# Attention output copied out of its banks at once, with the reciprocals multiplied in later on GpSimd

## Chip, cores and metric

The kernel runs on one core of a Trainium2 chip. The metric is the device time of one execution in microseconds (us). Its engines are TensorE (PE), VectorE (DVE), ScalarE (ACT), GpSimd (POOL) and SyncE (SP); SP issues the DMAs. Matrix products are written to banks of PSUM, from which VectorE and ScalarE copy to SBUF.

## What is computed

Three layers follow one another: causal attention with a decay (4 batches, 8 heads, 576 positions, head size 64), a gated feed-forward layer (MoE1), and a routed layer of eight experts (MoE2). The change is in the attention:

```
scores = scale * np.matmul(q, k.transpose(0, 1, 3, 2))
log_f = np.log(np.clip(f, 0.0001, 1.0))
cum = np.cumsum(log_f, axis=-1)
decay = cum[:, :, :, None] - cum[:, :, None, :]
scores = np.where(causal, -1000000000.0, scores + decay)
scores = scores - np.max(scores, axis=-1, keepdims=True)
attn = np.exp(scores)
attn = attn / (np.sum(attn, axis=-1, keepdims=True) + 1e-09)
return np.matmul(attn, v).astype(np.float32)
```

## The kernel before

**Tiles and pairs.** The 32 heads of all batches are worked off as 16 pairs p (`NP`); the two heads of a pair lie on the two halves of the partitions. The 576 query rows of a head are cut into five tiles i (one of 64 rows and four of 128). The pair loop in `run` is a pipeline: while pair p is transposed and multiplied by v, the scores of pair p + 1 are made.

**One iteration.** It goes through four groups g. `tr(p, g, a)` transposes exponentials of head a into a bank `ps_t` (two buffers) and copies them to `ath`, on ScalarE for a = 0 (L174) and on VectorE for a = 1 (L172). The transposes are L157 in group 0, L160 in group 1, L163 and L164 in group 2, L168 and L169 in group 3. Between the groups, `qk(p + 1, i)` makes scores (L134), takes their row maximum on VectorE (L138) and the exponential with row sums on ScalarE (L145), and `av(p, g - 1)` (L184) multiplies by v into the two accumulating banks `avx` (512 columns) and `avy` (64 columns), of which there is one buffer each. `rb(p)` adds 1e-9 to the row sums (L190) and takes reciprocals (L191). They are needed along the free dimension of the output, which holds queries, so `rt(p)`, in group 1, transposes them on PE (L196), copies them (L198), writes them to DRAM (`rd`, L201) and reads them back spread over 64 partitions per head as `rb` (L203).

**End of a pair.** `xout(p)` multiplies both banks by `rb` on VectorE (L210, L211) and writes the product over `rb`. GpSimd then rounds it to `xth` (L213) and takes the remainder `xtl` (L214), the two parts that MoE1 reads.

**Other work in the loop.** From pair 5 on, every second pair decodes a sixth of MoE1's first weight group (`decode`: L285 on ScalarE, L286 to L288 on VectorE, L291, L292, L297 and L300 on GpSimd). In the last pair the decode of the next group begins, with its steps on VectorE (L294) and ScalarE (L299) where it has no GpSimd engine given. `decay`, ahead of the loop, computes the logarithms and their running sum and splits 8 times the sum into three bf16 parts `pc`, whose DMAs `dq` and `dk` feed the second product of L134.

**Order.** PE's order in the attention is that of the program (`manual_schedule(engines={PE})`). The order on the other engines is set by a scheduler when the program is built. Each engine then works strictly in its order.

Of the kernel before, what the change touches and what calls it, by code (L numbers as in the profile page):

```python
# [9 lines left out]
F32 = mybir.dt.float32  # L10
# [3 lines left out]
ACTF = mybir.ActivationFunctionType  # L14
ALU = mybir.AluOpType
# [4 lines left out]
B, H, S, D = 4, 8, 576, 64  # L20
# [15 lines left out]
class Attention:  # L36
# [46 lines left out]
    def decay(self, ft, cum, one, pc):  # L83
        nc = self.nc
        pc = pc.rearrange("p (r s) -> p r s", r=3)
        nc.vector.tensor_scalar(ft, ft, 0.0001, 1.0, op0=ALU.max, op1=ALU.min)
        nc.scalar.activation(ft, ft, ACTF.Ln)
        nc.vector.tensor_tensor_scan(cum, one, ft, 0.0, op0=ALU.mult, op1=ALU.add)
        nc.scalar.activation(ft[:1, :1], ft[:1, :1], ACTF.Exp)
        nc.vector.tensor_scalar_mul(cum, cum, 8.0)  # L90
        for r in range(3):
            nc.vector.tensor_copy(pc[:, r], cum)
            if r < 2:
                nc.vector.tensor_sub(cum, cum, pc[:, r])
        dq, dk = self.dec[0]
        nc.sync.dma_start(out=dq[61:67], in_=pc[:2])
        for a, o in enumerate((58, 67)):
            nc.sync.dma_start(out=dk[o:o + 3], in_=pc[a:a + 1])
        nc.sync.dma_start(out=self.cd, in_=pc)
# [105 lines left out]
    def xout(self, p):  # L205
        nc = self.nc
        ax, ay = self.X
        b, f = divmod(p, 4)
        xt = self.rbt
        nc.vector.tensor_mul(xt[:, 64:], ax, xt[:, 64:])  # L210
        nc.vector.tensor_mul(xt[:, :64], ay, xt[:, :64])  # L211
        sl = slice(b * S, (b + 1) * S)
        nc.gpsimd.tensor_copy(self.xth[:, f, sl], xt)  # L213
        nc.gpsimd.tensor_sub(self.xtl[:, f, sl], xt, self.xth[:, f, sl].bitcast(F32))  # L214
# [760 lines left out]
```

## Time and profile before

| | |
|---|---|
| three runs | 1047.93, 1048.97 and 1053.7 us |
| the profiled execution | 1053.49 us, span 1051.3 us |
| PE busy | 971.3 us, 92% of the span |
| VectorE busy | 604.6 us, 58% |
| ScalarE busy | 414.2 us, 39% |
| GpSimd busy | 208.6 us, 20% |
| mean granted TensorE clock | 0.963 of full speed |

The span runs from the first to the last instruction. Attention takes up about the first 265 us of it, MoE1 the stretch to about 740, MoE2 the rest. A granted clock of 1 is 2.4 GHz, one of 0.5 is 1.2 GHz. A busy share is a mean over all stages; what holds up one stage is seen in the waits and in the timeline of that stage.

### The profile page before, as it was taken

To read this page: it belongs to the slowest core of one execution; us is meant where nothing else is said; L and a number is where in the kernel's file an instruction comes from. 1 tells how busy PE (TensorE), PEld (TensorE's weight loads), DVE (VectorE), ACT (ScalarE), POOL (GpSimd) and SP (SyncE) were. 2 spreads that over 40 slices of the span, in tenths; PEclk is the share of its full clock that TensorE was granted. 3 is DMA by queue.
4 is the path that set the end of the run, shared out by engine and by line. 5 is a ranking of instruction groups with operands and counts; after the bars stand their busy time and mean duration, and the time that the engine had idled before them with its cause. 6 is when DMAs were issued, how large, how long until landed. Compare 5 with 4: busy or idle time off the path is not lost.

```text
span 1051.3 us, 16223 instructions
## 1 busy us (share of the span) xinstructions
PE 971.3 (92%) x6122; PEld 840.1 (80%) x6122; DVE 604.6 (58%) x1436; ACT 414.2 (39%) x903; POOL 208.6 (20%) x190
## 2 busy tenths in 40 slices
PE   4998898998999999999999999999899999879893
PEld 2544444444889999999999999989799999879693
DVE  4565655657763845945846645667775555442731
ACT  3655564554333412312313212333364544343631
POOL 1013222323210200201101100000125444532011
PEclk9998998889999999999999999999899999989997
DMA  6123222311220300201201100011485565652300
GB/s 200 64 88 108 95 98 84 114 57 53 72 61 21 101 1 23 98 1 41 80 1 61 41 1 1 31 51 52 154 273 172 188 208 190 221 185 68 114 38 27
DMA packets 53118, 92.93 MB, mean 88 GB/s; under 512 B 6032, under 2 KB 26894, under 8 KB 53039
## 3 DMA queue, kind: packets, MB, share of 16 engines
q1 hardware_dynamic: 47535, 77.70, 23.3%
q0 software_dynamic: 5504, 14.17, 3.9%
q8 instruction: 49, 0.80, 0.3%
q14 instruction: 30, 0.25, 0.1%
HBM read 82.19 MB, written 10.16 MB: 88 GB/s over the span
## 4 chain that ended last, share of the span: by engine, by line
PE 45%; issue 18%; DMA 12%; DVE 10%; POOL 9%; ACT 3%; SPq 0%; POOLq 0%; DVEq 0%; ACTq 0%
PE ps_g L336 21%; PE ps_y L354 12%; DMA rb<-rd 8%; PE ps_s L134 4%; PE avx L184 2%; POOL out L671 2%; DVE dt L287 2%; POOL gate L611 2%; POOL w L300 1%; POOL yg L611 1%; POOL b_r L611 1%; ACT e L145 1%; DVE ds L294 1%; DVE dt L288 1%; DMA rd<-rt 1%
## 5 line engine op out<-in xcount | busy, mean ns | idle before, releaser
L336 PE MATMUL ps_g<-xth,w 128*128 128x384 f32 (+1 forms) x1184 | 309.8, 332 | 1.5 <-DVE hs L341 1.5
L336 PEld LDWEIGHTS ps_g<-xth,w 128*128 128x128 f32 x1184 | 213.5, 188 | 2.8 <-DVE hs L341 2.2
L336 PE MATMUL ps_g<-xtl,w 128*128 128x384 f32 (+1 forms) x592 | 196.5, 332 | 0.0
L354 PE MATMUL ps_y<-hh,w 128*128 128x384 f32 (+1 forms) x592 | 161.1, 333 | 3.7 <-DVE y L360 2.1
L145 ACT ACTIVATE e<-e,mx 128x320 f32<-128x320 f32 (+4 forms) x160 | 88.2, 552 | 85.7 <-DVE mx L138 84.6
L630 PE MATMUL m_psg<-ygh,w 128*128 128x304 f32 x512 | 117.0, 310 | 1.6 <-ACT b_o L780 1.2
L645 PE MATMUL m_psy<-h2h,w 128*128 128x304 f32 x512 | 114.6, 306 | 0.0
L354 PEld LDWEIGHTS ps_y<-hh,w 128*128 128x128 f32 x592 | 107.1, 188 | 6.7 <-DVE y L360 3.9
L336 PEld LDWEIGHTS ps_g<-xtl,w 128*128 128x128 f32 x592 | 111.5, 188 | 0.1
L300 POOL TENSOR_TENSOR w<-ds,w 128x512 fp32r<-128x512 f32 x36 | 49.8, 1383 | 275.4 <-ACT w L299 274.9
L557 DVE TENSOR_TENSOR w<-raw,w 128x1024 fp32r<-128x1024 f32 x64 | 76.6, 1221 | 38.3 <-ACT w L556 22.7
L354 PE MATMUL ps_y<-hl,w 128*128 128x384 f32 (+1 forms) x296 | 97.9, 331 | 0.1
L343 ACT ACTIVATE hh<-hs 128x384 fp32r<-128x384 f32 (+1 forms) x74 | 38.2, 516 | 133.8 <-DVE hs L342 133.8
L341 DVE SCALAR_TENSOR_TENSOR hs<-hs,ps_g 128x384 f32<-128x384 f32 (+1 forms) x74 | 39.9, 540 | 87.1 <-ACT hs L340 87.1
L630 PEld LDWEIGHTS m_psg<-ygh,w 128*128 128x128 f32 x512 | 87.0, 192 | 2.1 <-ACT b_o L780 1.3
L645 PEld LDWEIGHTS m_psy<-h2h,w 128*128 128x128 f32 x512 | 85.5, 188 | 0.3
L134 PE MATMUL ps_s<-qk 64*128 64x288 f32 (+4 forms) x384 | 76.5, 471 | 5.6 <-DMA qk<-qk 5.3
L556 ACT ACTIVATE w<-raw 128x1024 fp32r<-128x1024 f32 x64 | 67.4, 1058 | 33.2 <-PE m_psg L630 13.0
L340 ACT ACTIVATE hs<-ps_g 128x384 f32<-128x384 f32 (+1 forms) x74 | 35.5, 479 | 109.1 <-PE ps_g L336 109.0
L630 PE MATMUL m_psg<-ygl,w 128*128 128x304 f32 x256 | 78.2, 305 | 0.2 <-DVE ygl L598 0.2
L138 DVE CUSTOM_DVE_ANT_0 e<-ps_s,mask 128x320 f32<-128x320 f32 (+4 forms) x160 | 62.5, 426 | 27.6 <-PE ps_s L134 25.7
L360 DVE TENSOR_TENSOR y<-ps_y,y 128x384 f32<-128x384 f32 (+1 forms) x124 | 67.0, 541 | 19.1 <-PE ps_y L354 18.2
(300 smaller groups left out, 1513.6 us busy)
## 6 DMA issues: line engine op xcount, KB each, us to landing
raw<-w SPq DMA_DIRECT2D x64, 512.0 KB
qk<-qk SPq DMA_DIRECT2D x16, 576.0 KB
raw<-mg SPq DMA_DIRECT2D x12, 512.0 KB
raw<-mv SPq DMA_DIRECT2D x12, 512.0 KB
raw<-mo SPq DMA_DIRECT2D x12, 512.0 KB
v<-vL SPq DMA_DIRECT2D x16, 320.0 KB
rb<-rd SPq DMA_DIRECT2D x16, 288.0 KB
yd<-yr SPq DMA_DIRECT2D x18, 256.0 KB
```

The lines of the kernel that those rows point to most:

```text
L134: nc.tensor.matmul(ps[a][b:, :n], x[s, q0:w], y[s, lo:hi], start=c == 0, stop=c == 1, tile_position=(64 * a, b))
L138: nc.vector.tensor_tensor_reduce(out=es[a][b:, lo:hi], in0=ps[a][b:, :n], in1=mask[b:, off + lo:off + hi], scale=-0.125, scalar=BIGF if pr ...
L145: nc.scalar.activation(es[a][b:, :w], es[a][b:, :w], ACTF.Exp, bias=prev[a][b:], scale=-1.0, accum_out=rs[b:, c:c + 1])
L300: nc.gpsimd.tensor_sub(lo, s3, hi.bitcast(F32))
L336: nc.tensor.matmul(ps[:, :n], w[:, k, fs], x[:, k], start=(k == 0 and c == 0), stop=(k == 3 and c == 2))
L354: nc.tensor.matmul(ps[:, :n], w[:, f, ds], h[:, f, :n], start=(f == 0 and c == 0), stop=(f == 1 and c == 2))
L360: nc.vector.tensor_add(y, ps[:, :n], y)
L556: nc.scalar.activation(hi, r, ACTF.Copy)
L557: nc.vector.tensor_sub(lo, r, hi.bitcast(F32))
L611: self.pmark = self.nc.gpsimd.indirect_dma_start(out=dst, out_offset=None, in_=src[:, :], in_offset=bass.IndirectOffsetOnAxis(ap=ix, axis= ...
L630: nc.tensor.matmul(ps[:, :C], w[:, k, fs], x[:, k], start=(k == 0 and c == 0), stop=(k == 3 and c == 2))
L645: nc.tensor.matmul(self.P[e][d][:, :C], w[:, f, ds], h[:, f], start=(u == 0 and f == 0 and c == 0), stop=(u == 3 and f == 1 and c == 2))
```

## The change

`xout` no longer multiplies out of the banks. ScalarE copies `avx` and VectorE copies `avy`, unnormalised, into a tile `xt` of its own, and GpSimd multiplies `xt` by `rb` before it rounds and subtracts as before. The pool of `rb` also holds `xt`, two buffers each. In `decay` the scaling by 8 is merged into the split, which takes four VectorE operations in place of six.

```
-        nc.vector.tensor_scalar_mul(cum, cum, 8.0)
-        for r in range(3):
-            nc.vector.tensor_copy(pc[:, r], cum)
-            if r < 2:
-                nc.vector.tensor_sub(cum, cum, pc[:, r])
+        nc.vector.tensor_scalar_mul(pc[:, 0], cum, 8.0)
+        nc.vector.scalar_tensor_tensor(cum, cum, 8.0, pc[:, 0], op0=ALU.mult, op1=ALU.subtract)
+        nc.vector.tensor_copy(pc[:, 1], cum)
+        nc.vector.tensor_sub(pc[:, 2], cum, pc[:, 1])
...
-        xt = self.rbt
-        nc.vector.tensor_mul(xt[:, 64:], ax, xt[:, 64:])
-        nc.vector.tensor_mul(xt[:, :64], ay, xt[:, :64])
+        xt = self.xp.tile([128, S], F32, name="xt")
+        nc.scalar.activation(xt[:, 64:], ax, ACTF.Copy)
+        nc.vector.tensor_copy(xt[:, :64], ay)
+        nc.gpsimd.tensor_mul(xt, xt, self.rbt)
```

The first place where the order on an engine changes is VectorE at the program's start; `dec_cum` and `dec_pc` are `decay`'s tiles, `uo` holds constants that `Consts.load` casts (L830, L831).

```order
 L88 SCALAR_TENSOR_TENSOR dec_cum<-dec_one,dec_ft 32x576
-L90 TENSOR_SCALAR dec_cum<-dec_cum 32x576
+L90 TENSOR_SCALAR dec_pc<-dec_cum 32x576
+L91 SCALAR_TENSOR_TENSOR dec_cum<-dec_cum,dec_pc 32x576
 L92 CAST dec_pc<-dec_cum 32x576
-L94 TENSOR_TENSOR dec_cum<-dec_cum,dec_pc 32x576
-L92 CAST dec_pc<-dec_cum 32x576
-L94 TENSOR_TENSOR dec_cum<-dec_cum,dec_pc 32x576
+L93 TENSOR_TENSOR dec_pc<-dec_cum,dec_pc 32x576
 L830 CAST uo<-cst 128x128
 L831 CAST uo<-cst 128x128
-L92 CAST dec_pc<-dec_cum 32x576
```

The decay's last operation stood behind the two casts of constants and now stands ahead of them.

The second place is GpSimd in a pair with a decode step, with the output of the pair ahead between the decode's operations. Before:

```order
L291 TENSOR_SCALAR ds<-ds 128x512
L213 CAST xth<-rb 128x576
L214 TENSOR_TENSOR xtl<-rb,xth 128x576
L292 TENSOR_TENSOR ds<-ds,dt 128x512
L297 CAST w_1115<-ds 128x512
L300 TENSOR_TENSOR w_1116<-ds,w_1115 128x512
```

And in the change (lines behind L89 have numbers smaller by one, up to `xout`):

```order
L291 TENSOR_SCALAR ds<-ds 128x512
L211 TENSOR_TENSOR xt<-xt,rb 128x576
L292 TENSOR_TENSOR ds<-ds,dt 128x512
L213 CAST xth<-xt 128x576
L297 CAST w_1123<-ds 128x512
L214 TENSOR_TENSOR xtl<-xt,xth 128x576
L300 TENSOR_TENSOR w_1124<-ds,w_1123 128x512
```

The new product stands ahead of the decode's product L292, and the rest of the output's operations come between the decode's.

The third place is VectorE in the last pair, from the end of the pair ahead of it; `ath` is group 0 of the last pair at 64x512, group 1 at the first 128x512, group 2 at the second. Before:

```order
L287 SCALAR_TENSOR_TENSOR dt<-raw,dt 128x512
L210 TENSOR_TENSOR rb<-avx,rb 128x512
L211 TENSOR_TENSOR rb<-avy,rb 128x64
L288 SCALAR_TENSOR_TENSOR dt<-raw,dt 128x512
L190 TENSOR_SCALAR r<-rs_138 128x10
L172 COPY ath_2863<-ps_t 64x512
L191 RECIPROCAL rr_140<-r 128x10
L172 COPY ath_2877<-ps_t 128x512
L286 TENSOR_SCALAR dt<-raw 128x512
L287 SCALAR_TENSOR_TENSOR dt<-raw,dt 128x512
L288 SCALAR_TENSOR_TENSOR dt<-raw,dt 128x512
L172 COPY ath_2902<-ps_t 128x512
```

And in the change:

```order
L287 SCALAR_TENSOR_TENSOR dt<-raw,dt 128x512
L210 COPY xt<-avy 128x64
L288 SCALAR_TENSOR_TENSOR dt<-raw,dt 128x512
L189 TENSOR_SCALAR r<-rs_138 128x10
L171 COPY ath_2891<-ps_t 64x512
L190 RECIPROCAL rr_140<-r 128x10
L286 TENSOR_SCALAR dt<-raw 128x512
L287 SCALAR_TENSOR_TENSOR dt<-raw,dt 128x512
L171 COPY ath_2905<-ps_t 128x512
L288 SCALAR_TENSOR_TENSOR dt<-raw,dt 128x512
L294 SCALAR_TENSOR_TENSOR ds<-ds,dt 128x512
L171 COPY ath_2930<-ps_t 128x512
```

L286 and L287 of the next group's decode moved ahead of the copy of group 1, and L294 ahead of that of group 2; in every pair the two products of `xout` gave way to the copy of 64 columns. On ScalarE the copy of `avx` stands in every pair behind the last exponentials and ahead of group 0's copy to `ath`. PE's order in the attention is the same.

## Rows read from the trace of the kernel before

**Rows 1.** The page's chain that ended last: share of the span by engine and line.
```profile
PE ps_g L336 21%; PE ps_y L354 12%; DMA rb<-rd 8%; PE ps_s L134 4%; PE avx L184 2%; POOL out L671 2%; DVE dt L287 2%; POOL gate L611 2%; POOL w L300 1%; POOL yg L611 1%; POOL b_r L611 1%; ACT e L145 1%; DVE ds L294 1%; DVE dt L288 1%; DMA rd<-rt 1%
```

**Rows 2.** Waits, 28 to 270: who waited for whom, total us, times, longest.
```profile
DVE rb L210 <- DMA rb<-rd: 20.1, 9, 4.8
...
PE ps_t L160 <- DVE ath L172: 17.6, 10, 2.8
```

**Rows 3.** Timeline, 43 to 57: start, us, instructions in one row [idle before <-releaser].
```profile
43.29 0.27 PE L196 MATMUL ps_t<-cst,rr 128*32 128x128 f32 x1 [0.41 <-ACT ath L174]
...
51.70 1.06 PE L157 MATMUL ps_t<-cst,e 128*64 128x128 f32 x8
...
52.42 0.59 ACT L174 ACTIVATE ath<-ps_t 64x512 f32<-64x512 f32 x1 [0.39 <-PE ps_t L157]
...
53.00 0.69 DVE L210 TENSOR_TENSOR rb<-avx,rb 128x512 f32<-128x512 f32 x1 [1.60 <-DMA rb<-rd]
...
54.06 0.62 DVE L172 COPY ath<-ps_t 64x512 f32<-64x512 f32 x1
...
54.74 0.66 PE L160 MATMUL ps_t<-cst,e 128*128 128x128 f32 x4 [0.51 <-DVE ath L172]
```

**Rows 4.** Timeline of PE: L196 first and last, one late pair, pairs 14 and 15.
```profile
28.95 0.28 PE L196 MATMUL ps_t<-cst,rr 128*32 128x128 f32 x1
...
98.35 0.65 PE L160 MATMUL ps_t<-cst,e 128*128 128x128 f32 x4 [2.17 <-DVE ath L172]
...
237.26 1.06 PE L157 MATMUL ps_t<-cst,e 128*64 128x128 f32 x8
...
239.13 1.09 PE L160 MATMUL ps_t<-cst,e 128*128 128x128 f32 x8
...
241.50 0.28 PE L196 MATMUL ps_t<-cst,rr 128*32 128x128 f32 x1
...
249.92 1.06 PE L157 MATMUL ps_t<-cst,e 128*64 128x128 f32 x8
...
253.91 0.28 PE L196 MATMUL ps_t<-cst,rr 128*32 128x128 f32 x1 [0.39 <-DVE rr L191]
```

**Rows 5.** Windows: length, busy us per engine, granted clock, DMA share, GB/s.
```profile
29.02:253.91 224.89, 204.66 (x1360) 106.69 (x1360) 135.45 (x494) 125.19 (x377) 58.42 (x51) 0.92 0.25 84
99.00:108.00 9.00, 9.00 (x34) 4.02 (x35) 3.50 (x12) 3.28 (x10) 3.27 (x4) 0.50 0.19 69
...
300.00:720.00 420.00, 417.76 (x2428) 410.27 (x2427) 252.02 (x497) 117.72 (x227) 33.50 (x24) 1.00 0.11 35
```

**Rows 6.** Groups by line, ScalarE and GpSimd, 28 to 270: busy us, mean ns.
```profile
L174 ACT ACTIVATE ath<-ps_t 128x512 f32<-128x512 f32 x32 | 18.8, 587 | 12.8 <-PE ps_t L160 7.3 <-PE ps_t L164 5.0
...
L214 POOL TENSOR_TENSOR xtl<-rb,xth 128x576 fp32r<-128x576 f32 x15 | 21.1, 1407 | 1.2
...
L291 POOL TENSOR_SCALAR ds<-ds 128x512 f32<-128x512 f32 x6 | 10.2, 1702 | 49.0 <-ACT ds L285 49.0
```

**Rows 7.** L190 and L213: ns minimum, median, maximum; first and last start.
```profile
L190 DVE TENSOR_SCALAR r<-rs x16: 153/163/633, 25.5 to 252.5; 128x10 f32<-128x10 f32 x16
...
L213 POOL CAST xth<-rb x16: 658/663/1053, 40.2 to 269.6; 128x576 fp32r<-128x576 f32 x16
```

**Rows 8.** Timeline of the start, 11 to 16.
```profile
11.63 0.23 DVE L830 CAST uo<-cst 128x128 fp32r<-128x128 f32 x1 [3.38 <-DMA cst<-cst]
...
15.22 0.89 PE L134 MATMUL ps_s<-dk,dq 64*128 64x320 bf16 x2 [8.52 <-DMA dk<-dec_pc]
```

**Rows 9.** Timeline of the last pair, 255 to 272.
```profile
256.85 1.59 POOL L300 TENSOR_TENSOR w<-ds,w 128x512 fp32r<-128x512 f32 x1
...
259.70 0.69 PE L168 MATMUL ps_t<-cst,e 128*128 128x128 f32 x2 [2.47 <-ACT ath L174]
```

**Rows 10.** Chain that ended last, 140 to 250: start, us.
```profile
149.13 9.20 DMA rb<-rd
...
243.38 7.70 DMA rb<-rd
```

## Prediction

> **What bounds the kernel now.** I read the chain of work that ended last first. It is mostly TensorE (PE), but the transfer `rb<-rd`, the reciprocals on their way back from DRAM, holds 8% of the span [rows 1]. A DMA on that chain means that an engine stood still for it, so the list of waits for the attention stage comes next. VectorE's L210, the first product of `xout`, waited for that transfer in 9 of 16 pairs, 20.1 us in all, and PE's L160 (the transposes of group 1) waited in 10 pairs for VectorE's copy L172, 17.6 us in all [rows 2]. The timeline joins the two. In pair 2 the first transposes start at 51.70; L210 starts at 53.00 after 1.60 us of waiting, L172 stands behind it in VectorE's order and starts only at 54.06, and the second half of L160 starts at 54.74 after 0.51 us [rows 3]. So the wait costs PE time because L172 empties the bank that L160 needs, and L172 is queued behind `xout`.
>
> What a pair costs without it is read where the reciprocals were not late. From L157 of pair 14 (237.26) to its L196 (241.50) are 4.24 us, with L160 in one piece, and from that L196 to the next L157 (249.92) are 8.42 us [rows 4]. The second distance is the same in a pair that waits (43.29 to 51.70, 8.41) [rows 3]; the first is where all waiting lies. One undisturbed pair is thus 4.24 + 8.42 = 12.66 us.
>
> The waits cost more than their length. Behind a 2.17 us wait at 98.35 [rows 4], PE's granted clock is 0.50 from 99 to 108, its lower level of 1.2 GHz; over the attention stage the mean granted clock is 0.92, although PE is busy for 204.66 of 224.89 us [rows 5]. From 300 to 720 PE is busy for 417.76 of 420 us at full clock [rows 5]: nothing there absorbs an earlier arrival, it only moves.
>
> **The change, part by part.**
>
> *The pair loop.* The first L196 stands at 28.95 and the last at 253.91 [rows 4], 224.96 us for 15 periods. In the change VectorE has only the copy of `avy`, which waits for PE and not for a DMA; the product that needs `rb` is GpSimd's. If no wait is left, 14 periods take 12.66 us, and the last one I leave at what it takes now, 241.50 to 253.91, 12.4 [rows 4]. That is 177.2 + 12.4 = 189.6 us, a gain of 35.3 us. About half of it is waits and half is TensorE time at the lower clock that follows them.
>
> What hides the added work: ScalarE copies `avx`, 128x512, at 0.59 us each (the like copy L174 [rows 6]). It stands between the last exponentials and the copy L174 of group 0. In pair 2 ScalarE sat idle for 0.39 us there, L174 ran from 52.42 to 53.01 [rows 3], and L160 first needs that bank about 1.87 us behind the first transposes (237.26 to 239.13 [rows 4]), so at 53.57. The copy pushes L174 back by some 0.2 us, and 0.56 are free: price nothing. Without that cover it would be 0.59 us in each of 15 pairs, 9 us. VectorE saves L210's 0.69 us and keeps a copy of 64 columns. GpSimd's product, 128x576 with two operands in SBUF, I take from L214 with the same shape, 1.41 us [rows 6]; a pair then holds 1.41 + 0.66 (the cast L213 [rows 7]) + 1.41 = 3.5 us of GpSimd work, and the decode of weights, in every second pair from pair 5 on, adds four operations, the longest of them L291 with 1.70 us [rows 6], so at most 6.8: under 10.3 in 12.66. The late reciprocals now make GpSimd wait, and who waits for GpSimd? `xth` and `xtl` are read first in the MoE stage, and the two buffers of `xt` come free two pairs later.
>
> The Trainium skill speaks against this choice of engine: "GPSIMD Engine Reference", section "Engine selection", sends elementwise products of two inputs to VectorE and calls GpSimd about twice as slow. The trace agrees (1.41 us beside 0.69 for 512 of the columns). By that rule alone the change would lose some 0.7 us a pair, 11 us in all; it does not decide here, as GpSimd has room in each pair.
>
> *The start.* The decay's arithmetic loses two VectorE operations, but what counts is the order: now its last cast (L92) stands behind two casts of constants, the first of which waited 3.38 us, until 11.63, for the transfer of constants, and PE's first product with the decay starts at 15.22 behind the DMA that follows [rows 8]. In the change all of the decay stands ahead of those casts. The gain is at most 3.4 us, and at least nothing (its small transfers may queue behind the loads of q, k and v already requested). Neither end is nearer by a row; I take the middle, 1.7.
>
> *The last pair and the hand-over.* Here VectorE's order puts two operations of the next weights' decode (L286, L287) ahead of the copy of group 1. L286 waits until GpSimd has read the buffer it writes, and that GpSimd step stands behind the new product. Then, as now, the copies of group 2 hang on GpSimd's L300: it ran to 258.44, and PE's L168 started at 259.70 after 2.47 us of waiting [rows 9]; the first transposes of this pair were at 249.92. The chain ahead of L300 is in the change: reciprocals, product, decode product, two casts, two differences, all of it still about 8 to 10 us behind the first transposes, where it is 8.5 now. Behind the last pair GpSimd's chain from the reciprocals to `xtl` is 1.41 us longer, in place of L210's 0.69 on VectorE. I take 1.5 us of loss, between a gain of 0.5 and a loss of 3.
>
> **Sum.** -35.3 - 1.7 + 1.5 = -35.5 us. The profiled execution took 1053.5, so 1018.0. It lies 4.5 us above the median of the three runs shown (1048.97) and beside the slowest of them; if part of that was waits in attention, which then vanish in both, the changed kernel stays at 1018, and if it was anything else, its median is near 1013.5. I take 1016.
>
> **Rivals.**
>
> *GpSimd and VectorE get in each other's way.* VectorE's L190 takes 163 ns in the median but up to 633, and GpSimd's cast L213 663 but up to 1053: the long ones are where both ran at the same time, behind the decode steps [rows 7]. In five decode pairs L190 ends about 1.5 us behind the first transposes, with L172 behind it. The reciprocals land there 1.2 to 2.7 us behind them: requested 1.88 us behind L196 (243.38 less 241.50), less the 8.42, plus 7.70 to 9.20 of travel [rows 4, 10]. If the product starts first, L190 waits for up to 1.41 us and L160 for about 1.1. With all five that is 5.5 us lost; with the uncovered ScalarE copy in part, up to 12: 1022 to 1030. The Trainium skill, "SBUF — State Buffer", section "Who interferes with whom", says that the two engines share one pair of ports, that whichever issues first holds it for its whole instruction, and that the other is blocked; the slow L190 and L213 agree with that.
>
> *The clock falls anyway.* If smaller gaps that remain are enough to keep the lower clock, only the waits of L160 (17.6) and the start come back: 1053.5 - 17.6 - 1.7 = 1034, or 1030 by the median. Against it: the rows show the lower clock behind a wait of 2.17 us, and the gaps that remain are shorter than 0.4.
>
> *Slower.* GpSimd becomes the bound. With two `xt` buffers, ScalarE's copy waits for GpSimd once the GpSimd work of a pair exceeds the pair, and L174, L160 and PE stand behind it. This decides when GpSimd needs more than the present mean of 15.0 us a pair (224.96 / 15); I count 3.5, and up to 10.3 with a decode, about 6 in the mean. Were VectorE to block the product until it took 12 us in place of 1.41, the mean would be 16.6: 1.6 us more in each of 15 pairs, 1078. Nothing among the rows comes near: the longest stretch of a blocked GpSimd operation is 0.39 us (1053 less 663 [rows 7]).
>
> *No change.* The gain is given back at the hand-over, since the weights of MoE's second group are decoded late: then some 1050 to 1053. It would need a wait of 35 us, where PE now has 2 idle us in 420 [rows 5].
>
> **How the numbers follow.** The likeliest case, 1010 to 1022, has 0.62; engines in each other's way, 1022 to 1030, 0.20; the clock, 1030 to 1043, 0.12; no change 0.03; slower 0.03. About half a per cent, 5 us, is what a measurement of this kernel can tell from no change. The range of 8 in 10 takes the first two cases and the bounds of the start and the hand-over (3.4 and 0.5 better): 1007 to 1030. Faster 0.94, same 0.03, slower 0.03.
>
> **What would show it.** Right: L196 to L196 at 12.7 us in all pairs but the first and last; no wait of L160 for L172 over 0.3 us; granted clock 1.00 between the start and the last pair; GpSimd, not VectorE, waiting for `rb<-rd`; PE's first product with the decay at about 13.5. Wrong: L190 of 1 us or more with L160 late behind it (first rival); full pairs but half clock (second); ScalarE's copy waiting for GpSimd (slower); or a PE gap of more than 5 us at the hand-over.

## The result, and the profile after

The changed kernel takes 1019.96 us (median of 4 runs, 1019.65 to 1021.13), the kernel before 1050.0 beside it: ratio 0.971, 95% interval 0.968 to 0.974, so 2.9% faster. The forecast was 1016, with a range of 1007 to 1030. The profiled execution took 1019.87 us, 33.6 less than that of before, which the sum had put at 35.5.

The loop of pairs first. PE's timeline, with the transpose of reciprocals (L195 now, L196 before) in the pairs that answer to [rows 3] and at both ends of the loop:

```profile
26.53 0.28 PE L195 MATMUL ps_t<-cst,rr 128*32 128x128 f32 x1
...
39.28 0.27 PE L195 MATMUL ps_t<-cst,rr 128*32 128x128 f32 x1 [0.23 <-ACT ath L173]
...
49.56 1.09 PE L159 MATMUL ps_t<-cst,e 128*128 128x128 f32 x8
...
51.92 0.28 PE L195 MATMUL ps_t<-cst,rr 128*32 128x128 f32 x1
...
203.88 0.28 PE L195 MATMUL ps_t<-cst,rr 128*32 128x128 f32 x1
...
215.25 0.28 PE L195 MATMUL ps_t<-cst,rr 128*32 128x128 f32 x1
```

From L195 to L195 every period is 12.64 to 12.75 us but the last, 11.37, and L159 runs in one piece of eight. The windows of the loop and of the stretch behind it (length, busy us of PE, its weight loads, VectorE, ScalarE, GpSimd, granted clock, DMA):

```profile
26.53:215.25 188.72, 186.73 (x1359) 100.53 (x1359) 126.19 (x478) 131.94 (x392) 75.06 (x65) 1.00 0.30 101
215.25:300.00 84.75, 76.37 (x421) 70.56 (x421) 43.37 (x68) 28.56 (x58) 18.15 (x14) 0.96 0.17 53
```

The loop of 224.96 us is now 188.72, a gain of 36.24. PE's busy time for the same products fell by some 18 us (204.66 in [rows 5]) at a clock of 1.00 in place of 0.92, and its idle time by as much. The waits, 26 to 270 (us in all, times, longest), answer to [rows 2]:

```profile
POOL xt L211 <- DMA rb<-rd: 24.3, 3, 10.3
```

VectorE no longer waits for the transfer; GpSimd does. PE's wait at L159 for VectorE's copy is gone from the list. By line, ns minimum, median, maximum, first and last start:

```profile
L189 DVE TENSOR_SCALAR r<-rs x15: 164/173/175, 35.3 to 213.4; 128x10 f32<-128x10 f32 x15
...
L211 POOL TENSOR_TENSOR xt<-xt,rb x16: 1403/1410/1420, 36.9 to 231.5; 128x576 f32<-128x576 f32 x16
...
L213 POOL CAST xth<-xt x16: 657/662/669, 38.4 to 233.0; 128x576 fp32r<-128x576 f32 x16
```

None of them has the long ones of [rows 7]. The start, answering to [rows 8]: PE's first product with the decay comes 1.92 us earlier, and the cast of constants, which still waits, stands in nobody's way.

```profile
11.77 0.23 DVE L830 CAST uo<-cst 128x128 fp32r<-128x128 f32 x1 [3.20 <-DMA cst<-cst]
...
13.30 0.50 PE L133 MATMUL ps_s<-dk,dq 64*128 64x320 bf16 x2 [6.77 <-DMA dk<-dec_pc]
```

The last pair and the hand-over, answering to [rows 9] (SPq is SP's queue, which requests the transfers):

```profile
218.87 0.90 PE L162 MATMUL ps_t<-cst,e 128*128 128x128 f32 x3 [1.74 <-DVE ath L171]
...
222.36 0.52 SPq L202 DMA_DIRECT2D rb<-rd  x1
...
231.47 1.42 POOL L211 TENSOR_TENSOR xt<-xt,rb 128x576 f32<-128x576 f32 x1 [10.33 <-DMA rb<-rd]
...
235.16 0.63 ACT L299 ACTIVATE w<-ds 128x512 fp32r<-128x512 f32 x1 [7.76 <-POOL xtl L214]
...
237.72 0.51 ACT L343 ACTIVATE hh<-hs 128x384 fp32r<-128x384 f32 x1
...
239.87 0.69 PE L336 MATMUL ps_g<-xth,w 128*128 128x384 f32 x1 [4.71 <-DVE hs L341]
```

GpSimd stands 10.33 us for the last reciprocals. They are requested only at 222.36, 7.11 us behind L195 (5.78 in the kernel before, where the request is at 259.69; 1.88 in a pair without this delay): in SP's order a load of weights (L279, at 221.86) stands ahead of the request, and it waits for ScalarE's L285, which waits for GpSimd's L300. ScalarE's decode (L299, L285) then stands for GpSimd, and MoE1's gating (L343, then L340) stands behind the decode in ScalarE's order, so PE waits 4.71 us. In the kernel before L343 stood ahead of that L285 (272.34 and 273.84).

### The profile page after: what moved, and what is told of

Its sections match the earlier page's. It is cut to its first block, busy times and chain, and to the rows that moved or that the text cites. A ratio compares the mean times of both kernels' runs of the same rounds, so it can differ in the third digit from the quotient of the medians.

```text
span 1018.1 us, 16252 instructions
## 1 busy us (share of the span) xinstructions
PE 952.0 (94%) x6122; PEld 833.6 (82%) x6122; DVE 594.1 (58%) x1418; ACT 421.2 (41%) x919; POOL 228.5 (22%) x206
## 4 chain that ended last, share of the span: by engine, by line
PE 54%; issue 19%; POOL 9%; DVE 8%; ACT 4%; DMA 4%; POOLq 0%; SPq 0%; DVEq 0%; ACTq 0%
PE ps_g L336 22%; PE ps_y L354 12%; PE avx L183 5%; PE ps_s L133 5%; POOL out L671 2%; DVE dt L287 2%; POOL gate L611 2%; POOL yg L611 2%; POOL w L300 1%; PE ps_t L156 1%; PE ps_t L159 1%; ACT e L144 1%; DMA raw<-w 1%; PE ps_t L162 1%; PE ps_t L167 1%
## 5 line engine op out<-in xcount | busy, mean ns | idle before, releaser
L336 PE MATMUL ps_g<-xth,w 128*128 128x384 f32 (+1 forms) x1184 | 310.4, 332 | 5.0 <-DVE hs L341 5.0
L336 PEld LDWEIGHTS ps_g<-xth,w 128*128 128x128 f32 x1184 | 214.0, 189 | 6.4 <-DVE hs L341 5.7
L336 PE MATMUL ps_g<-xtl,w 128*128 128x384 f32 (+1 forms) x592 | 196.6, 332 | 0.0
L300 POOL TENSOR_TENSOR w<-ds,w 128x512 fp32r<-128x512 f32 x36 | 50.4, 1399 | 275.1 <-ACT w L299 275.1
L336 PEld LDWEIGHTS ps_g<-xtl,w 128*128 128x128 f32 x592 | 111.7, 189 | 0.0
L343 ACT ACTIVATE hh<-hs 128x384 fp32r<-128x384 f32 (+1 forms) x74 | 38.2, 516 | 136.8 <-DVE hs L342 136.8
L340 ACT ACTIVATE hs<-ps_g 128x384 f32<-128x384 f32 (+1 forms) x74 | 35.4, 478 | 104.8 <-PE ps_g L336 104.7
L645 PE MATMUL m_psy<-h2l,w 128*128 128x304 f32 x256 | 77.4, 302 | 0.0
L133 PE MATMUL ps_s<-qk 64*128 64x288 f32 (+4 forms) x384 | 70.1, 437 | 5.4 <-DMA qk<-qk 5.1
```

What stands on the lines that cost most here:

```text
L133: nc.tensor.matmul(ps[a][b:, :n], x[s, q0:w], y[s, lo:hi], start=c == 0, stop=c == 1, tile_position=(64 * a, b))
L300: nc.gpsimd.tensor_sub(lo, s3, hi.bitcast(F32))
L336: nc.tensor.matmul(ps[:, :n], w[:, k, fs], x[:, k], start=(k == 0 and c == 0), stop=(k == 3 and c == 2))
L645: nc.tensor.matmul(self.P[e][d][:, :C], w[:, f, ds], h[:, f], start=(u == 0 and f == 0 and c == 0), stop=(u == 3 and f == 1 and c == 2))
```

## The experiments

Chips differ (the kernel before has medians of 1038.9 to 1055.9 on them), so the times are read as ratios to the kernel before on the same chip, and from each run's own rows. The loop is always counted from the first transpose of reciprocals to the last, 188.72 us in the changed kernel.

**Each part alone.** Of the diff of the change, only `xout`:

> Only the part of the change in xout; the decay's pieces are made as before. Theory (the loop's gain and the start's gain are separate, and the loop's is nearly all of it): the first transpose of reciprocals comes about 1.9 us later than in the changed kernel, the loop keeps its even period of 12.66 us, the time is 1022 us (1020.5 to 1023.5). Rival (the earlier start sets the phase at which the loads arrive, so that without it some pairs wait again): over 1026 us, with waits of TensorE at L159 or L162 in the loop.

and only `decay`:

> Only the new decay; xout as before. Theory: the start is about 1.9 us earlier and the loop as in the kernel before, with VectorE waiting for rb<-rd some 20 us in all and TensorE for ath some 17 us behind it: 1048 us (1046 to 1050). Rival (the start's shift takes the waits away by moving the loads against the reciprocals): below 1040 us.

Ratios 0.971 (0.968 to 0.974) and 0.996 (0.994 to 0.999). Windows of the loop, first of `xout` alone, then of the decay alone:

```profile
28.93:217.68 188.75, 186.72 (x1361) 100.53 (x1359) 126.30 (x478) 131.97 (x392) 75.07 (x65) 1.00 0.30 100
```

```profile
26.89:252.77 225.88, 206.45 (x1362) 107.14 (x1361) 134.88 (x495) 124.98 (x377) 58.41 (x51) 0.92 0.25 84
```

The loop's gain is wholly `xout`'s. The start shows in the rows (first transpose at 28.93 and 26.89), but 2 us are below what the ratio can tell.

**The product on VectorE, banks released as in the change.**

```
-        nc.gpsimd.tensor_mul(xt, xt, self.rbt)
+        nc.vector.tensor_mul(xt, xt, self.rbt)
```

> As the changed kernel, banks copied out at once, but VectorE makes the product in place in one instruction of 128x576 and no longer GpSimd. In VectorE's order this product stands behind the copy of the next pair's group 0 and ahead of its row maxima, so a DMA that comes late holds VectorE again, but one copy later than before. Theory (what counts is which queue stands waiting for the DMA, not the banks): VectorE waits for rb<-rd again in several pairs, TensorE waits behind it, and the time lies between the two kernels, 1024 to 1042 us. Rival (the early release of the output banks is what helps): 1020 us plus at most 2.

Ratio 0.978 (0.973 to 0.982), 1016.6 us on a chip where the kernel before takes 1038.9. The expected 1024 to 1042 were meant beside 1050, a ratio of 0.975 to 0.992, which holds it; the rival's (0.973 at most) is at the interval's edge, so the rows decide. The loop took 201.47 us. VectorE's timeline, PE's, and PE's windows:

```profile
144.95 0.76 DVE L211 TENSOR_TENSOR xt<-xt,rb 128x576 f32<-128x576 f32 x1 [2.60 <-DMA rb<-rd]
```

```profile
89.41 0.66 PE L159 MATMUL ps_t<-cst,e 128*128 128x128 f32 x4 [1.99 <-DVE ath L171]
...
146.43 0.98 PE L159 MATMUL ps_t<-cst,e 128*128 128x128 f32 x4 [2.83 <-DVE ath L171]
```

```profile
76.47:91.14 14.67, 12.68 (x94) 1.00 0.36 122
118.45:130.91 12.46, 12.46 (x94) 1.00 0.32 88
130.91:149.51 18.60, 14.09 (x93) 0.92 0.33 104
```

With the banks out early but the wait on VectorE, the chain of [rows 3] is back in five pairs, and the loop is 12.8 us longer than the changed kernel's: early release alone does not do it. Still, 23.5 of the 36.2 us come back in this run. In VectorE's order the product now stands behind the copy of group 0, so the transfer has longer to arrive: VectorE waits 9.7 us for it in the loop, where the kernel before has 15.4 (its 20.1 [rows 2] hold 4.8 behind the loop). The run by itself doesn't part this from the earlier release; but in the kernel before no product into the output banks (L184) waits for VectorE, so their late release held up nothing there. The even period is 12.46 us and not 12.66; that is taken up below.

**VectorE's work without the wait.** Products as in the kernel before, with the reciprocals of the pair ahead:

```
+        self.rbo = self.rbt if p else None
         rb = self.rbt = self.xp.tile([128, S], F32, name="rb")
...
+        rb = self.rbo if p else self.rbt
+        nc.vector.tensor_mul(xt[:, 64:], ax, rb[:, 64:])
+        nc.vector.tensor_mul(xt[:, :64], ay, rb[:, :64])
```

> The new decay, and the products on VectorE straight from the banks as in the kernel before, but each pair is multiplied by the reciprocals of the pair ahead (this part of the computation is changed), which have long arrived: no copies out of the banks, no product on GpSimd, and no instruction of VectorE that waits for the late DMA. Theory (the wait for the DMA in VectorE's queue was the cost): the even period of 12.66 us, or up to 0.3 us more since VectorE has 0.7 us more work ahead of the copy of group 0; 1017 to 1024 us. Rival (VectorE's 0.9 us of products, or the banks held until then, were the cost): 1040 us or more.

Ratio 0.996, which looks like the rival, but the rows say otherwise. Window of the loop, and a row of PE's timeline near the end:

```profile
26.79:220.07 193.28, 188.12 (x1361) 100.44 (x1361) 135.82 (x493) 124.93 (x377) 58.75 (x51) 1.00 0.31 98
```

```profile
999.32 1.09 PE L764 MATMUL m_pst<-cst,b_y 128*128 128x128 f32 x4 [12.11 <-DMA b_y<-yd,b_d]
```

The loop takes 193.28 us at full clock, but the altered attention sends tokens elsewhere, and the loop over surplus blocks (L764), which the changed kernel's trace does not have at all, runs near the end. So its total prices nothing. I therefore kept the change whole and added the old work to VectorE:

```
+        self.rbo = self.rbt if p else None
         rb = self.rbt = self.xp.tile([128, S], F32, name="rb")
...
         nc.gpsimd.tensor_mul(xt, xt, self.rbt)
+        if p:
+            z = self.xp.tile([128, S], F32, name="z")
+            nc.vector.tensor_mul(z[:, 64:], ax, self.rbo[:, 64:])
+            nc.vector.tensor_mul(z[:, :64], ay, self.rbo[:, :64])
```

> The changed kernel in full, and VectorE besides makes the two products of the kernel before out of the banks, into a scratch tile that nobody reads, by the reciprocals of the pair ahead, which have long arrived. So VectorE has its old work of 0.9 us a pair again and the banks are held for it again, ahead of or right behind the copy of group 0, but nothing on VectorE waits for the late DMA. Theory (the wait was the cost, not the work nor the banks): the period stays at 12.7 us, up to 0.3 us more in some pairs, the time within 4 us of the changed kernel on this chip. Rival (the work or the banks were the cost): 15 us or more above it.

1020.01 us beside 1025.51 of the changed kernel on the same chip, 5.5 less where at most 4 either way were expected. In the profiles MoE1's gating ends at 705.2 and 705.6, so the 5.5 us lie behind it, in work that the edit doesn't touch, and the loop decides. Its window, PE's longest wait for VectorE in it, and what stood ahead of that wait on GpSimd and VectorE:

```profile
26.36:217.01 190.65, 187.55 (x1361) 1.00 0.31 100
```

```profile
88.72 0.66 PE L159 MATMUL ps_t<-cst,e 128*128 128x128 f32 x4 [1.30 <-DVE ath L171]
```

```profile
86.64 1.40 POOL L212 TENSOR_TENSOR xt<-xt,rb 128x576 f32<-128x576 f32 x1 [1.41 <-DMA rb<-rd]
...
86.81 1.26 DVE L189 TENSOR_SCALAR r<-rs 128x10 f32<-128x10 f32 x1
```

Neither VectorE's 0.9 us a pair nor the banks, held until VectorE has read them, cost more than 5 us in the loop (190.65 less the 185.8 of a loop at 12.46 throughout, below). What cost was the wait. Some 2.6 of these 5 us lie in two periods (13.97 and 13.58 us) in which L189 took 1.26 and 0.90 us where 0.16 is its median here: GpSimd's product had started ahead of it, and L189 ended with the product. This is the first rival of the prediction, and it is taken up again below.

**GpSimd loaded.** Two more products a pair, with `z` a scratch tile:

```
+        if p + 1 < NP:
+            z = self.xp.tile([128, S], F32, name="z")
+            for _ in range(2):
+                nc.gpsimd.tensor_mul(z, xt, self.rbt)
```

> The changed kernel with two more products of 128x576 on GpSimd in each pair but the last, into a scratch tile that nobody reads: 2.8 us more on GpSimd per pair of 12.66 us. Theory (GpSimd has room: it is busy 75 of 189 us): the period stays 12.66 us and the time within 2 us of the changed kernel, 1019 to 1022 us. Rival (GpSimd is near its limit or slows VectorE's work while it runs): 1025 us or more, with TensorE waiting in the loop for VectorE's ath or for GpSimd's xt.

1017.08 us, ratio 0.963 (0.956 to 0.970). Window of the loop:

```profile
27.02:215.74 188.72, 186.74 (x1360) 100.52 (x1360) 126.13 (x478) 131.98 (x392) 113.04 (x93) 1.00 0.30 101
```

38 us more of GpSimd work, and neither the loop nor VectorE's busy time moves: GpSimd had room for the product three times over.

The run serves below as the yardstick on its chip, and its hand-over is not that of the changed kernel. SP requests the last reciprocals ahead of the load of weights, 2.15 us behind the last transpose of reciprocals (215.74):

```profile
217.89 0.52 SPq L202 DMA_DIRECT2D rb<-rd  x1
```

PE waits 2.54 us at L162, but at the gating 0.4 us in all and not 4.71, with the same order on ScalarE. That points to the late request as the main part of the 4.71. From the last transpose of reciprocals to the end of MoE1's gating this run takes 486.5 us, the changed kernel 489.7.

**What a late copy costs.** Three runs made group 0's copies late in pairs 5, 7, 9, 11 and 13. First, VectorE's copy six times over:

```
-            self.mark[1] = nc.vector.tensor_copy(th[:np_, :n], tp[:np_, :n])
+            for _ in range(6 if g == 0 and p in (5, 7, 9, 11, 13) else 1):
+                self.mark[1] = nc.vector.tensor_copy(th[:np_, :n], tp[:np_, :n])
```

> The changed kernel, but in pairs 5, 7, 9, 11 and 13 VectorE makes its copy of group 0 six times over instead of once (five more of 0.68 us): the copy is 3.4 us late in five pairs, as it was in the kernel before behind the late reciprocals. Some 0.75 us of that is hidden, so TensorE waits some 2.6 us at L159 or L162 in each of the five. Theory (a wait of this size costs its own length and about as much again, because the granted clock falls behind it): 18 to 28 us more, 1038 to 1048 us, with stretches at a granted clock of 0.5 behind each wait. Rival (a wait costs its length alone): 10 to 14 us more, 1030 to 1034 us.

1038.19 us beside 1017.08 of the run with GpSimd loaded, 21 more; the loop 205.85, 17.1 more, and 3.5 more at the hand-over, where the yardstick is ahead. PE's windows over one late pair and the next, and over the last late pair and the one behind it; then its longest wait in the last late pair:

```profile
90.65:118.57 27.92, 26.34 (x182) 1.00 0.33 108
188.60:203.83 15.23, 12.74 (x91) 1.00 0.26 79
203.83:220.68 16.85, 16.71 (x92) 0.80 0.05 18
```

```profile
203.83 0.28 PE L196 MATMUL ps_t<-cst,rr 128*32 128x128 f32 x1 [1.74 <-DVE ath L172]
```

The time met the theory's range, but not by its mechanism: the row maxima went between the six copies, and four of five late pairs cost 2.60 us (27.92 less twice 12.66) at full clock. Only the last, with a wait of 1.74 (and one of 0.75 ahead of it, as in the others), cost 6.76 (15.23 + 16.85 less 25.32), 4.2 of it in a pair at a clock of 0.80. It differed by the same meeting of GpSimd and VectorE as above: L190 started at 198.49, just behind GpSimd's product at 198.43, and took 1.37 us, so that all six copies came later. One long copy instead:

```
+            src = tp[:np_, :n]
+            if g == 0 and p in (5, 7, 9, 11, 13):
+                z = self.ap.tile([64, 5, 512], BF16, name="z", bufs=1)
+                long = nc.vector.tensor_copy(z, src.unsqueeze(1).to_broadcast([64, 5, 512]))
...
```

The copy to `ath` is issued behind it.

> The changed kernel, but in pairs 5, 7, 9, 11 and 13 VectorE first runs one long copy of group 0 (five times its 512 columns, into a scratch tile that nobody reads), so that its own copy of group 0 comes some 3.2 us later in one piece. TensorE then has one wait of 2 to 2.6 us in each of the five, where the six short copies of the run before left it three waits of 0.25 to 0.75 us. Theory (a wait of over 2 us costs its length and about as much again through the granted clock): the period with the long copy and the one behind it together 5 to 6 us over 25.3, the loop 24 to 30 us longer, with stretches at a granted clock of 0.5 behind each wait. Rival (the length alone): 2.0 to 2.6 us for each, the loop 10 to 13 us longer, the clock 1.00.

The loop took 192.52 us, 3.8 more, and the time is that of the changed kernel (1024.49 beside 1025.51). VectorE's row and PE's wait:

```profile
88.24 2.81 DVE L174 CAST z<-ps_t 64x2560 bf16<-64x2560 f32 x1
```

```profile
90.25 0.66 PE L159 MATMUL ps_t<-cst,e 128*128 128x128 f32 x4 [0.75 <-ACT ath L180]
```

A miss: by its releaser, the second half of group 1 now took the bank that ScalarE's copy frees, not VectorE's, so that 2.81 us cost 0.75. Then both copies were made late:

```
+        if g == 0 and p in (5, 7, 9, 11, 13):
+            z = self.ap.tile([64, 4, 512], BF16, name=f"z{a}", bufs=1)
+            src = tp[:64].unsqueeze(1).to_broadcast([64, 4, 512])
+            long = [nc.vector.tensor_copy(z, src) if a else nc.scalar.activation(z, src, ACTF.Copy)]
...
```

> The changed kernel, but in pairs 5, 7, 9, 11 and 13 both ScalarE and VectorE first run a long copy of group 0 (four times its 512 columns, into scratch tiles that nobody reads), so that neither bank of group 0 comes free in time for the transposes of group 1; with VectorE's copy late alone, the run before took the bank of ScalarE instead and lost 0.75 us. TensorE should have one wait of 1.5 to 2.2 us in each of the five pairs, with shorter ones behind it. Theory (the granted clock falls behind a wait of this size, so that it costs about twice its length or more): the pair with the long copies and the one behind it together 4 to 7 us over 25.3, the loop of 188.7 us longer by 20 to 35 us, granted clock 0.80 to 0.90 over the pair behind each. Rival (the length alone): 2 to 3 us for each, the loop 10 to 15 us longer at a clock of 1.00.

Ratio 0.979 (0.974 to 0.983). Window of the loop, and the waits in one late pair:

```profile
25.81:225.19 199.38, 187.84 (x1359) 1.00 0.29 95
```

```profile
88.20 0.66 PE L159 MATMUL ps_t<-cst,e 128*128 128x128 f32 x4 [1.31 <-ACT ath L181]
89.60 0.66 PE L159 MATMUL ps_t<-cst,e 128*128 128x128 f32 x4 [0.75 <-ACT ath L181]
```

10.7 us more, 2.1 a late pair: the length of the waits and no more, at a clock of 1.00. Here the rival holds. My rule that such a wait costs twice its length is not general.

**A better version.** The weights of MoE1's second group decoded one chunk later, behind the first gating:

```
...
-                        if g < 5 and t0 == 0 and f == 0:
+                        if 0 < g < 5 and t0 == 0 and f == 0:
...
+                        if g == 0 and t0 == CH[1][0] and f == 0:
+                            wts.pools = [wab[1]]
+                            with tc.issue_after(m1.mark[0].ins), tc.issue_after(m1.mark[1].ins):
+                                m1.load(1)
```

> The changed kernel with the second group of expert weights decoded one chunk later: its ScalarE, VectorE and GpSimd work stands behind the first chunk's gating instead of in the last pair and ahead of it. Theory (the hand-over loses time because ScalarE stands at L285 for GpSimd, which stands at L211 for the last pair's reciprocals, with the gating's L340 and L343 behind it): TensorE's waits of 1.74 us at L162 and 4.71 us at L336 shrink to below 1 us each and the two stretches of half clock behind them go; 1012 to 1017 us. Rival (the hand-over waits for the last pair's xth and xtl whatever stands ahead, or the weights then come late for the second group): 1019 us or more.

1010.09 us beside 1017.08 (GpSimd loaded) on the same chip, below the expected 1012 to 1017. PE's window behind the loop:

```profile
216.00:300.00 84.00, 82.99 (x478) 1.00 0.21 66
```

The waits at L162 and L336 are gone and the clock stays up, as the theory had it. From the last transpose of reciprocals to the end of the gating it takes 478.9 us, 7.6 less than with GpSimd loaded and 10.8 less than the changed kernel. The request for the last reciprocals comes 2.06 us behind L195 here, so the run takes away SP's order and ScalarE's at once and does not part them. The last 0.2 us a pair are in ScalarE's order. First the changed kernel, then the product on VectorE:

```profile
76.07 0.54 ACT L144 ACTIVATE e<-e,mx 128x320 f32<-128x320 f32 x1
...
76.62 0.57 ACT L173 ACTIVATE ath<-ps_t 128x512 f32<-128x512 f32 x1
```

```profile
75.05 0.60 ACT L173 ACTIVATE ath<-ps_t 128x512 f32<-128x512 f32 x1 [1.18 <-PE ps_t L159]
```

The copy of group 1, whose bank L195 needs (0.23 us of waiting at 39.28, above), stands behind two exponentials in the one and ahead of them in the other. Moved ahead, with the later weights kept:

```
...
+                    if nx and g == 1:
+                        with self.tc.issue_after(self.mark[0].ins):
+                            self.later()
```

where `later` holds the exponentials of the 320-wide tile.

> The weights of the second group decoded one chunk later (as in e6_load_later), and in each pair ScalarE's copy of the next group 1 stands ahead of the two exponentials of the 320-wide tile instead of behind them. Theory (the transpose of reciprocals starts 0.2 us late in each period, since it needs the bank that this copy frees, and the product on VectorE, where the copy already stood ahead, had a period of 12.46 us): period 12.46 instead of 12.66 us, 2.8 us less in the loop, and with the hand-over's 7 us some 9 to 10 us below the changed kernel on the same chip. Rival (the 0.2 us come from something else, or the exponentials come late for their transposes instead): the period stays 12.6 us or more and the gain is the hand-over's 6 to 8 us alone.

> The changed kernel itself, as the yardstick on the chip on which the three other kernels of this call run, since chips differ by up to 10 us in a stretch of the second expert layer. Ratio to the kernel before 0.963 to 0.974; the loop of fifteen pairs takes 188.7 us from the first transpose of reciprocals to the last, the first product of the first expert layer's output (ps_y) starts 217 us after the first transpose of reciprocals.

Ratios 0.954 (0.950 to 0.958) and, for the changed kernel again, 0.973 (0.968 to 0.978): 1003.48 and 1025.51 us. PE's window of the loop in the better version:

```profile
26.90:212.68 185.78, 185.78 (x1362) 1.00 0.31 102
```

The period is 12.46 us (the last 11.39) and PE is busy for all of the loop. Of the 22 us between the two, the loop gives 2.9. The products of MoE1's gating and of MoE2's first layer show the rest: first the changed kernel again, then the better version.

```profile
L336 PE MATMUL ps_g<-xth,w x240: 277/334/422, 601.7 to 705.6; 128*128 128x384 f32 x72, 128*128 128x256 f32 x48
```

```profile
L630 PE MATMUL m_psg<-ygh,w x512: 296/302/602, 728.8 to 998.2; 128*128 128x304 f32 x171
```

```profile
L344 PE MATMUL ps_g<-xth,w x208: 276/334/423, 600.1 to 691.6; 128*128 128x384 f32 x56, 128*128 128x256 f32 x48
```

```profile
L638 PE MATMUL m_psg<-ygh,w x512: 296/302/602, 714.9 to 976.4; 128*128 128x304 f32 x171
```

At the end of the gating it is 14.0 us ahead (2.9 from the loop, 10.6 from the hand-over, 0.5 from ahead of the loop), and 8 more come from MoE2 (269.4 and 261.5 us), which neither edit touches. Those 8 are not claimed for the edits.

## Why the prediction was right

*What bounded the kernel.* Shown: over the loop of the changed kernel (188.72), VectorE's work costs 36 us with the wait (224.96) and 2 without it (190.65); with the banks out early but the wait on VectorE, 13 (201.47). The last two runs have the even period of 12.46, so that beside a loop at 12.46 throughout (185.8) they are 5 and 16 us longer.

*The loop, forecast -35.3, measured -36.24.* The 14 periods are the 12.66 that were forecast; the last came out at 11.37 and not 12.4, since it too had held a wait (0.39 us at L196 [rows 4]) and one product of MoE1 more; the rest of that 1.0 us stays open. Half the gain is idle time and half the clock, as forecast. But that a wait costs more than its length holds in the mean and not of each one: the prediction read the clock behind one wait, and behind another of the same trace it stayed up (the last section).

*ScalarE's copy at nothing.* L159 in one piece says that L173 was in time. The 0.2 us a period that ScalarE costs were there before: 12.66 was read from an undisturbed pair of the kernel before.

*GpSimd's product.* 1.41 us as forecast, hidden; VectorE makes the same product in 0.76 us (L211 above). The Trainium skill's rule ("GPSIMD Engine Reference", section "Engine selection") that GpSimd is about twice as slow at it agrees with these rows. It did not decide, as the product's wait and its work lie off the chain.

*The start, forecast -1.7.* The first decay product came 1.92 us earlier and the first transpose 2.42.

*The hand-over, forecast +1.5.* This was the mis-sized term. At the first transpose of reciprocals of the last pair the kernel is 38.66 us ahead, at the end of MoE1's gating 36.0 (740.9 in the kernel before, 704.9 now, rows below): a loss of 2.7. The prediction had looked at L168 and at GpSimd's chain behind the reciprocals, and left out how late these are requested. The wait at L168 (L167 now) has shrunk to 0.48 us, and the time is lost at L162, behind VectorE's decode, and at L336, by the late request and ScalarE's order. The new product stands ahead of L300 on GpSimd, L285 waits for L300, the load of weights for L285 and the request behind the load: so the request stands at 7.11 us and not 5.78. The run with GpSimd loaded, where the request is early, has 0.4 us in place of the 4.71; the run with the later weights shows that neither wait is left without this decode. How the 2.7 divide between SP's order and ScalarE's was not tested.

*From the sum to the forecast.* By the medians the gain is 30.0 us, by the profiled executions 33.6: that of the kernel before lay 3.5 above its median, that of the changed kernel on it. So 1018.0 was the nearer number, and the step from it to 1016 was not borne out. The lower end of the range, 1007, does not follow from its terms: 1016 with the better bounds of the start (1.7 less) and of the hand-over (2.0 less) is 1012.

*What the sum did not hold.* From the end of MoE1's gating to the end of the kernel another 2.4 us went. MoE2's first products take 264.2 us here (728.1 to 992.3), 261.9 before (764.0 to 1025.9) and 269.4 in a second profile of the same kernel: a spread that the change needn't explain. What sets it I did not test. The rows are these products by line, with their first start and last end, before and then after:

```profile
L336 PE MATMUL ps_g<-xth,w x335: 277/334/422, 599.9 to 740.9; 128*128 128x384 f32 x120, 128*128 128x256 f32 x48
...
L630 PE MATMUL m_psg<-ygh,w x512: 296/302/603, 764.0 to 1025.9; 128*128 128x304 f32 x171
```

```profile
L336 PE MATMUL ps_g<-xth,w x240: 277/334/422, 601.0 to 704.9; 128*128 128x384 f32 x72, 128*128 128x256 f32 x48
...
L630 PE MATMUL m_psg<-ygh,w x512: 296/302/601, 728.1 to 992.3; 128*128 128x304 f32 x171
```

*Rivals.* GpSimd and VectorE in each other's way: not in the loop of the changed kernel, where L189 stays at 175 ns at most; 38 us more of GpSimd work leave VectorE's busy time there unchanged. But it was near, and in part luck: in three of the six pairs with a decode the product starts only 0.2 to 0.3 us behind L189 (86.86 and 87.11 in the first). With VectorE 0.9 us later the product came first, L189 took 1.26 us, and PE waited 1.30, close to the 1.1 that the prediction gave it. The Trainium skill ("SBUF — State Buffer", section "Who interferes with whom") says that where the two engines contend for the ports that they share, the one that issues first blocks the other for its whole instruction. The row of 86.81 agrees: L189 ended with GpSimd's product. The clock falling anyway: no, 1.00. GpSimd as the bound: far off (75.06 us busy in 188.72). All given back at the hand-over: 2.7 of it.

## What to carry to other kernels

An instruction that waits for a late transfer costs what stands behind it on its engine. So look up whose queue it stands in before asking which engine does the work faster: here a product at half the speed on an engine that nobody waits for won 2.9%. Then look at the seam to the next stage, where that engine's lateness can come back through a third engine's order, the queue that requests the transfers included. There moving a load was worth 7 us beside the run with GpSimd loaded and by the rows 10.8 beside the changed kernel; in the loop itself 3 came from one copy moved ahead of two exponentials.

## What the runs showed that I had not expected

The length of a wait alone doesn't tell whether the clock falls. A wait of 1.74 us was followed by a pair at 0.80 (copies six times over), one of 1.99 by none (its pair, 76.47 to 91.14, ran at 1.00), 1.68 and 2.83 within one period (130.91 to 149.51) left it at 0.92, with 0.50 from 147.00 to 149.51, and 1.31 + 0.75 in a pair cost their length. The kernel before has both cases too: behind 2.17 us of waiting at 98.35 the clock is 0.50 from 99 to 108 [rows 5], behind 2.62 at 131.09 it stays at 1.00 (length, busy us of PE, its weight loads, VectorE, ScalarE, GpSimd, granted clock, DMA):

```profile
131.10:140.10 9.00, 9.00 (x59) 4.42 (x59) 6.15 (x24) 5.76 (x18) 3.92 (x4) 1.00 0.23 80
```

What else decides stays open.

A late copy can cost little if the other copy's bank is taken in its place: 2.81 us of VectorE's time cost PE 0.75.
